# Layer norm of three token blocks taken from the transposed input, and the first raw MLP weights loaded earlier

## The chip, the cores and the metric

The kernel runs on one core of a Trainium2 chip. The metric is device time in microseconds (us) of one execution; lower is better. Before the change three runs took 2244.16 to 2245.52 us, median 2245.15 us.

## The reference, cut to what matters

```python
x = A_x                                        # [2048, 576], fp32
g = sigmoid((x * gate_w).sum(-1))
q, k, v = split(x @ wqkv)                      # 32 heads of 18
a = softmax(q @ k.T * 18 ** -0.5) @ v @ wo
y = (x - mean(x)) / sqrt(var(x) + 1e-5)        # per token
b = gelu(y @ w1 + b1) @ w2 + b2                # 576 -> 4608 -> 576
out = g * a + (1 - g) * b
```

The change is about `y`, the normed input of the MLP, and about the first pieces of `w1` and `w2`.

## The kernel before, in words

Products keep fp32 accuracy by cutting each operand into a rounded high part and a rest (`hh`, `hl`; `big` holds both) and adding three matmuls of the parts.

The program has a first stage of some 215 us, a long loop, and a tail. **The first stage** goes over four blocks of 512 tokens (`tb` 0 to 3; here block 0 to block 3). Each block is a list of 17 groups, g0 to g16 (L872): nine `qk_group`s (L807, 14 matmuls of 128x512 each) and eight `v_group`s (L827, 14 matmuls of 128x288). A group fills one PSUM bank of the pool `ps_a`, which has four. ScalarE copies the bank to the high part, VectorE subtracts it to get the rest (L821, L822), and SyncE stores both.

Between groups, tables of numbers put the other work of the stage:

- `x_chunk` (L747): four transposes on TensorE (`transposed`, L739, one [128 x 128] tile for each 128 tokens), then ScalarE and VectorE make the parts of the transposed input of the *next* block. Five chunks, after g2 to g6.
- `norm` (L776): stages 0 and 1 make mean and variance on VectorE (L784, L785), and stage 1 the reciprocal of the deviation, with one square root on ScalarE (L790 to L797). Stages 2 and 3 sum x times the gate's weights (L802), and normalize the token rows in place (L804). In block 0 they stand after g5 to g8, in blocks 1 and 2 after g2 to g5, in block 3 after g0 to g3.
- `y_chunk` (L762): four more transposes of the normalized rows, then the parts of `y` (L766, L767), stored to `y_scr`. Five chunks, after g12 to g16 in block 0, g8 to g12 in blocks 1 and 2, g5 to g9 in block 3.
- In block 0 alone, the cutting of `wqkv` into parts (L736, L737), by VectorE or GpSimd.
- From block 1 on, the first score rounds of the attention (`next_round`, L223 and L225: a pair of rounds is four matmuls and four row maxima on VectorE), after the odd groups of block 2, for instance.

Each engine works through its instructions in the order in which the code issues them. So a transpose placed after a group runs on TensorE behind that group and ahead of the next one, and when its input isn't there yet, the next group waits with it.

**The raw MLP weights** are loaded by `load_w1` and `load_w2` into one input tile (L346 to L348). The first loads stand at the first `next` of the MLP's generator, after g2 of block 3. ScalarE and GpSimd cut them into parts (`split`, L376; L381 and L385) from g9 of block 3 on.

**The tail** multiplies the attention's output by `wo` in four blocks (L1123). Between its evictions (L1127), `PLAN` (L49) places the steps that scale the next block's output by its denominators: `normed` (L1032), with L1040 on VectorE as its first step.

Of the kernel before, what the change touches and what calls it, by code (L numbers as in the profile page):

```python
# [8 lines left out]
F32 = mybir.dt.float32  # L9
# [40 lines left out]
        [(0,), (1,), (2,), (3,), (4,), (5,), (6,), ()]]  # L50
# [7 lines left out]
N_AT = 5  # L58
W_AT = {0: 1, 1: 2, 2: 3, 4: 4, 6: 5, 7: 6}
# [6 lines left out]
def gated_mix_kernel(ctx: ExitStack, tc: tile.TileContext, x, wqkv, wo, w1, b1, w2, b2, gate_w, out):  # L66
# [17 lines left out]
    b_scr = dram.tile([S, D], F32, name="b_scr")  # L84

# [38 lines left out]
    def x_tile():  # L124
        return xp.tile([P, 4 * 640], F32, name="x")
# [206 lines left out]
    def mlp():  # L332
# [13 lines left out]
        raws = x_tile()  # L346
        R1 = raws[:, :9 * P].rearrange("p (c n) -> p c n", c=9)
        R2 = [raws[:, 9 * P + k * D:9 * P + (k + 1) * D] for k in range(2)]  # L348
# [3 lines left out]
        def load_w1(q):  # L352

            if (1, q) in LOADED or q >= NQ0:
                return
            LOADED[1, q] = slot[0] + LAND
            fc = chunk(q)[2]
            for h in range(2):
                src = w1[:, (fc + h) * P:(fc + h + 1) * P]
                nc.sync.dma_start(R1[64 * h:64 * h + 64], src.rearrange("(c p) n -> p c n", p=64))  # L360

        def load_w2(c):
            if (2, c) in LOADED or c >= NFC:
                return
            LOADED[2, c] = slot[0] + LAND
            nc.sync.dma_start(R2[c % 2], w2[c * P:(c + 1) * P, :])

# [37 lines left out]
        def prep(upto):  # L405

            while asked[0] <= min(upto, npair - 1):
                q = asked[0]
                asked[0] += 1
                shape = [P, 2, 9, P]  # L410
                if q >= NQ0:
                    reload(W1, q, wp1, shape, w1_scr[q % NQ0])
                    continue
                split(W1, q, wp1, shape, (1, q), R1, w1_scr[q], lambda q: load_w1(q + 1))

        def prep_w2(i):
            for m in range(G // 2):
                q = i * (G // 2) + m
                for j in range(2):
# [4 lines left out]
                    split(W2, (q, j), wp2, [P, 2, D], (2, c), R2[c % 2], w2_scr[c],  # L424
# [186 lines left out]
        load_w1(0)  # L611
        for c in range(2):
            load_w2(c)
# [79 lines left out]
    with ExitStack() as a:  # L693
# [10 lines left out]
        glog = wpool.tile([P, NT], F32, name="glog")  # L704

# [41 lines left out]
        def x_chunk(tb, c):  # L747
# [4 lines left out]
            ps = transposed(tb, c)  # L752
            if c < 4:
                nc.scalar.activation(big[:, c, :], ps, AF.Copy)
                nc.vector.tensor_tensor(big[:, 4 + c, :], ps, big[:, c, :].bitcast(F32), op=ALU.subtract)
            else:
# [3 lines left out]
                nc.vector.tensor_tensor(big[64:128, 8, :], ps[64:128], tmp[64:128, :].bitcast(F32), op=ALU.subtract)  # L760

        def y_chunk(tb, c):  # L762
# [5 lines left out]
            for s_, e in enumerate((eh, el)):  # L768
                if c < 4:
                    nc.sync.dma_start(y_scr[tb, s_, 2 * c:2 * c + 2].rearrange("c p n -> (c p) n"), e.bitcast(F32))  # L770
                else:
                    nc.sync.dma_start(y_scr[tb, s_, 8], e[0:64].bitcast(F32))
# [3 lines left out]
        def norm(tb, stage):  # L776
# [21 lines left out]
            if stage >= 2:  # L798
                junk = pp.tile([P, 2, 2, TB], F32, name="p").rearrange("p a b c -> p (a b c)")
                for t in (2 * stage - 4, 2 * stage - 3):  # L800
# [3 lines left out]
                    nc.vector.tensor_scalar(xv[:, t, :], xv[:, t, :], stats[:, tt, 0:1], rstds[tb][:, t:t + 1],  # L804
                                            op0=ALU.subtract, op1=ALU.mult)
# [56 lines left out]
        for i in range(2):  # L862
            for j in range(2):
                nc.gpsimd.memset(KA[i][64 * j + 32:64 * j + 64, :].bitcast(F32), 1.0)
        for c in range(5):
# [5 lines left out]
        for tb in range(NB):  # L871
            work = [(qk_group, (tb, mt)) for mt in (range(9) if tb < 2 else (4, 0, 1, 2, 3, 5, 6, 7, 8))] + [(v_group, (tb, t, n)) for t in range(4) for n in range(2)]  # L872
            for g, (fn, args) in enumerate(work):
# [12 lines left out]
                ng = g - (N_AT, 2, 2, 0)[tb]  # L886
                if 0 <= ng < 4:
                    norm(tb, ng)
                if tb + 1 < NB and 2 <= g < 7:
                    x_chunk(tb + 1, g - 2)  # L890
                yg = g - (12, 8, 8, 5)[tb]
                if 0 <= yg < 5:
                    y_chunk(tb, yg)
                if g == (16 if tb == 0 else 13) and tb + 2 < NB:
                    load_x(tb + 2)
# [342 lines left out]
```

## Time and profile before

| what | value |
|---|---|
| median of three runs | 2245.15 us |
| the profiled execution: its own time | 2244.72 us |
| its span, first to last instruction | 2242.9 us |
| TensorE matmul busy | 2220.6 us, 99% of the span |
| VectorE busy | 1648.7 us, 74% |
| ScalarE busy | 1425.8 us, 64% |
| GpSimd busy | 964.2 us, 43% |
| mean granted TensorE clock | 0.999 |

How to read the rows: PE is TensorE's matmuls, DVE is VectorE, ACT ScalarE, POOL GpSimd, SP SyncE. A row of a timeline has start and duration in us, the engine, the line, the operation, output and input, and in brackets how long the engine stood idle before it and what ended that. A row of the table of stretches has the stretch, its length, the busy time of each engine with the number of instructions, the granted clock (1.00 is full), the share of the DMA engines and GB/s. A row of the table of groups ends with the busy time in us and the mean ns of one.

### The profile page before, as it was taken

To read this page: it belongs to the slowest core of one execution; us is meant where nothing else is said; L and a number is where in the kernel's file an instruction comes from. 1 tells how busy PE (TensorE), PEld (TensorE's weight loads), DVE (VectorE), ACT (ScalarE), POOL (GpSimd) and SP (SyncE) were. 2 spreads that over 40 slices of the span, in tenths; PEclk is the share of its full clock that TensorE was granted. 3 is DMA by queue.
4 is the path that set the end of the run, shared out by engine and by line. 5 is a ranking of instruction groups with operands and counts; after the bars stand their busy time and mean duration, and the time that the engine had idled before them with its cause. 6 is when DMAs were issued, how large, how long until landed. Compare 5 with 4: busy or idle time off the path is not lost.

```text
span 2242.9 us, 51659 instructions
## 1 busy us (share of the span) xinstructions
PE 2220.6 (99%) x20585; PEld 1588.3 (71%) x20585; DVE 1648.7 (74%) x2892; ACT 1425.8 (64%) x2650; POOL 964.2 (43%) x970
## 2 busy tenths in 40 slices
PE   9999999999999999999999999999999999999998
PEld 7887667767666776676676766776766767776768
DVE  5677677777778777777777777777776777777734
ACT  4223677777776666666666666666666666666671
POOL 3001766666665444444444444444444444444700
PEclk9999999999999999999999999999999999999999
DMA  7757654445454624333354424232464334242264
GB/s 249 254 171 239 215 176 128 151 158 174 139 194 146 192 77 145 119 123 105 113 169 145 137 80 135 99 123 99 126 170 144 107 115 124 95 143 99 84 212 167
DMA packets 163624, 327.65 MB, mean 146 GB/s; under 512 B 56742, under 2 KB 83978, under 8 KB 152654
## 3 DMA queue, kind: packets, MB, share of 16 engines
q1 hardware_dynamic: 161286, 320.61, 44.1%
q8 instruction: 162, 2.65, 0.5%
q10 hardware_dynamic: 1968, 3.70, 0.4%
q14 instruction: 80, 0.66, 0.1%
q0 software_dynamic: 128, 0.03, 0.0%
HBM read 231.90 MB, written 96.16 MB: 146 GB/s over the span
## 4 chain that ended last, share of the span: by engine, by line
PE 92%; DVE 2%; DMA 2%; POOL 1%; ACT 1%; SPq 0%; issue 0%; ACTq 0%; DVEq 0%; POOLq 0%
PE ps L281 20%; PE ps L473 20%; PE ps L561 19%; PE ps L263 13%; PE ps L223 11%; PE ps L815 4%; PE ps L836 2%; PE ps L1123 2%; DVE m L225 1%; DMA x<-ot_scr 1%; PE ps L742 1%; DMA low<-ot_scr 0%; POOL zz L176 0%; ACT zz L526 0%; PE ps L818 0%
## 5 line engine op out<-in xcount | busy, mean ns | idle before, releaser
L225 DVE TENSOR_REDUCE m<-ps 128x1 f32<-128x512 f32 x2048 | 1312.3, 685 | 412.0 <-PE ps L223 387.9
L266 ACT ACTIVATE p<-ps 128x512 f32<-128x512 f32 x1368 | 741.2, 596 | 380.2 <-PE ps L263 376.3
L473 PE MATMUL ps<-big,w 64*128 64x512 f32 x3708 | 570.0, 393 | 1.8 <-ACT v L845 1.0
L176 POOL TENSOR_SCALAR zz<-zz 128x512 f32<-128x512 f32 x288 | 178.4, 620 | 752.4 <-ACT zz L526 730.3
L561 PE MATMUL ps<-w,hh 64*128 64x288 f32 x4352 | 485.7, 294 | 4.3 <-DVE x L578 2.4
L266 ACT ACTIVATE ring<-ps 128x512 f32<-128x512 f32 x680 | 369.1, 596 | 190.0 <-PE ps L263 188.4
L263 PE MATMUL ps<-qa,ka 56*128 56x512 f32 x2048 | 461.0, 422 | 2.9 <-ACT p L266 2.4
L561 PEld LDWEIGHTS ps<-w,hh 64*128 64x128 f32 x4352 | 425.6, 186 | 32.6 <-DVE x L578 4.9
L223 PE MATMUL ps<-ka,qa 54*128 54x512 f32 x2048 | 434.8, 398 | 0.7
L473 PEld LDWEIGHTS ps<-big,w 64*128 64x128 f32 x3708 | 370.9, 187 | 66.7 <-ACT v L845 1.3
L176 POOL TENSOR_TENSOR zz<-zz,z 128x512 f32<-128x512 f32 x288 | 371.8, 1291 | 24.0
L263 PEld LDWEIGHTS ps<-qa,ka 56*128 56x128 f32 x2048 | 214.4, 184 | 220.7 <-DVE m L225 180.6
L561 PE MATMUL ps<-w,hl 64*128 64x288 f32 x2176 | 349.2, 292 | 0.8 <-POOL hl L176 0.8
L281 PE MATMUL ps<-p,vt 128*32 128x512 f32 x2560 | 322.8, 598 | 0.0
L223 PEld LDWEIGHTS ps<-ka,qa 54*128 54x128 f32 x2048 | 219.1, 184 | 24.4 <-DVE m L225 3.8
L561 PEld LDWEIGHTS ps<-w,hl 64*128 64x128 f32 x2176 | 232.5, 185 | 1.2 <-POOL hl L176 1.1
L176 POOL TENSOR_TENSOR w<-x,w 128x576 fp32r<-128x576 f32 (+1 forms) x54 | 98.7, 1843 | 294.2 <-ACT w L381 275.0
L176 POOL TENSOR_TENSOR hl<-zz,hh 128x512 fp32r<-128x512 f32 x136 | 176.6, 1299 | 11.4
L281 PE MATMUL ps<-ring,vt 128*32 128x512 f32 x1280 | 168.5, 598 | 0.0
L281 PEld LDWEIGHTS ps<-p,vt 128*32 128x32 f32 x2560 | 67.0, 109 | 142.6 <-issue 136.4
L578 DVE SCALAR_TENSOR_TENSOR x<-ps,x 128x288 f32<-128x288 f32 x256 | 104.1, 448 | 9.6 <-PE ps L561 9.6
L815 PE MATMUL ps<-big,wqk 128*128 128x512 f32 x432 | 109.2, 401 | 0.4 <-DVE wqk L737 0.4
(114 smaller groups left out, 1468.3 us busy)
## 6 DMA issues: line engine op xcount, KB each, us to landing
w<-w_scr SPq DMA_DIRECT2D x54, 1152.0 KB
w<-w_scr SPq DMA_DIRECT2D x108, 576.0 KB
x<-in_B_w_dram SPq DMA_DIRECT2D x72, 288.0 KB
w_scr<-w SPq DMA_DIRECT2D x18, 1152.0 KB
w_scr<-w SPq DMA_DIRECT2D x36, 576.0 KB
qa<-qk_scr SPq DMA_DIRECT2D x192, 72.0 KB
ka<-qk_scr SPq DMA_DIRECT2D x84, 144.0 KB
qk_scr<-hh SPq DMA_DIRECT2D x36, 256.0 KB
```

What stands on the lines that cost most here:

```text
L176: fn(*args, **kw)
L223: nc.tensor.matmul(ps, qa[r0:r0 + 54, t * P:(t + 1) * P], ka[r0:r0 + 54, kb * TB:(kb + 1) * TB], start=True, stop=True)
L225: nc.vector.tensor_reduce(M4[u][:, h, t, kb:kb + 1], ps, axis=AX.X, op=ALU.max)
L263: nc.tensor.matmul(ps[h], ka[r0:r0 + 56, kc * P:(kc + 1) * P], qa[r0:r0 + 56, qb * TB:(qb + 1) * TB], start=True, stop=True)
L266: nc.scalar.activation(RING[n % 3][:, qb, h], ps[h], AF.Exp, scale=SCALE)
L281: nc.tensor.matmul(OB[u][r:r + 32, :], v[:, k, 19 * h:19 * h + 32], RING[c % 3][:, qb, h, :], start=(k == 0), stop=(k == NT - 1))
L473: nc.tensor.matmul(ps[h], wt[w_][r, c, :], y[r, c, :], start=(k == 0), stop=(k == 26))
L561: mm = nc.tensor.matmul(ps[nn][:, :ND], h_[r, tok], w_[p_][r, cs[nn]], start=(k == 0), stop=(k == 6 * G - 1))
L578: nc.vector.scalar_tensor_tensor(dst, ps[nn][:, :ND], 0.5, b2b[:, cs[nn]] if g == 0 else dst, op0=ALU.mult, op1=ALU.add)
L815: nc.tensor.matmul(ps, w_[:, c, ms], big[:, s_, :], start=(k == 0), stop=False)
L836: nc.tensor.matmul(ps[:, :ND], big[:, s_, tok], w_[:, c, cs], start=(k == 0), stop=False)
L1123: nc.tensor.matmul(ps[:, :ND], OT[b][2][:, s_, tok], w_part(w_, c)[:, cs], start=(k == 0), stop=(k == 13))
```

## The change

Block 0 keeps its way, but its five `y_chunk`s move from g12..g16 to g8..g12. For blocks 1 to 3 (one block ahead, that is in the groups of blocks 0 to 2):

- The normalization in place and the five second transposes go. Instead `x_chunk` takes the transposed tile in PSUM, subtracts a row of means on VectorE (line 773 of the changed kernel), and multiplies by a row of reciprocal deviations on GpSimd. Two or three groups later `y_parts` makes the parts, on ScalarE and GpSimd, and they are stored one group after that.
- The rows come from `stat_rows`: two small VectorE copies into `stp`, one TensorE transpose of `stp`, a ScalarE copy and a store to DRAM. `load_wide` then loads the rows back, spread over all partitions, into `QA[2]`, which isn't used yet.
- Statistics stand after g3 and g4 of block 0, and after g0 and g1 of blocks 1 and 2. `stat_rows` stands after g5 of block 0 and g2 of blocks 1 and 2. The `x_chunk`s stand after g12..g16 of block 0, and g5..g9 of blocks 1 and 2. Block 3 has none of this any more.
- The input of block 2 is loaded after g13 instead of g16 of block 0, that of block 3 after g0 instead of g13 of block 1.

The raw MLP weights get two input tiles, and the first four pieces of `w2` and two of `w1` are loaded after g11 of block 2. In the tail, the steps for the last block stand two evictions later.

```diff
 PLAN = [...
-        [(0,), (1,), (2,), (3,), (4,), (5,), (6,), ()]]
+        [(), (), (0,), (1,), (2,), (3,), (4,), (5, 6)]]
...
+BLOCK = [dict(stats=3, rows=5, wide=7, gate=9, x=12, lag=3, load=13),
+         dict(stats=0, rows=2, wide=3, gate=3, x=5, lag=2, load=0),
+         dict(stats=0, rows=2, wide=3, gate=3, x=5, lag=2)]
...
-        raws = x_tile()
+        for raws in (x_tile(), x_tile()):
...
-        load_w1(0)
-        for c in range(2):
-            load_w2(c)
+        for q in range(2):
+            load_w1(q)
+            for c in range(2 * q, 2 * q + 2):
+                load_w2(c)
+        yield 1
...
             ps = transposed(tb, c)
+            if tb > 0:
+                if c == 0:
+                    yT[tb] = pp.tile([P, 2, 2, TB], F32, name="p").rearrange("p a b c -> p (a b) c")
+                y = yT[tb][:, c % 4, :]
+                nc.vector.tensor_tensor(y, ps, wide[:, 0, :], op=ALU.subtract)
...
+            if tb > 0:
+                nc.gpsimd.tensor_tensor(y, y, wide[:, 1, :], op=ALU.mult)
...
+        def y_parts(tb, c):
+            y = yT[tb][:, c % 4, :]
+            eh = hp.tile([P, TB], F32R, name="hh")
+            el = hp.tile([P, TB], F32R, name="hl")
+            nc.scalar.activation(eh, y, AF.Copy)
+            nc.gpsimd.tensor_tensor(el, y, eh.bitcast(F32), op=ALU.subtract)
+            after(1, lambda: y_store(tb, c, eh, el))
...
+        def stat_rows(tb):
+
+            nc.vector.tensor_copy(stp[:, 0:4], stats[:, 4 * tb:4 * tb + 4, 0])
+            nc.vector.tensor_copy(stp[:, 4:8], rstds[tb])
+            ps = psum(ps_a)
+            nc.tensor.transpose(ps[:, :P], stp, ident)
+            nc.scalar.activation(strow, ps[:8, :P], AF.Copy)
+            nc.sync.dma_start(st_scr[tb], strow)
+
+        def load_wide(tb):
+            rows = bcast_rows(st_scr[tb], 8 * P)
+            nc.sync.dma_start(wide, rows.rearrange("p (a n) -> p a n", a=2))
...
-                    nc.vector.tensor_scalar(xv[:, t, :], xv[:, t, :], stats[:, tt, 0:1], rstds[tb][:, t:t + 1],
-                                            op0=ALU.subtract, op1=ALU.mult)
+                    if tb == 0:
+                        nc.vector.tensor_scalar(xv[:, t, :], xv[:, t, :], stats[:, tt, 0:1], rstds[tb][:, t:t + 1],
+                                                op0=ALU.subtract, op1=ALU.mult)
...
+                if tb == 0:
+                    if 0 <= g - N_AT < 4:
+                        norm(0, g - N_AT)
+                    if 0 <= g - 8 < 5:
+                        y_chunk(0, g - 8)
...
+                    if g in (at["stats"], at["stats"] + 1):
+                        norm(tb + 1, g - at["stats"])
+                    if g == at["rows"]:
+                        stat_rows(tb + 1)
```

How the instructions stand now. Names are as in the code, except that buffer numbers follow some of them (`wqk_125` is a part of the qk weights, `wv_127` of the v weights). The line numbers of the first list of each pair are those of the kernel before, of the second those of the changed one. First TensorE in block 0, from the end of g5 into g6; before, with a chunk of block 1's input between them:

```order
L815 MATMUL ps<-big,wqk_125 128x512
L817 MATMUL ps<-big,wqk_124 128x512
L818 MATMUL ps<-big,wqk_125 128x512
L742 MATMUL ps<-ident,x 128x128 x4
L815 MATMUL ps<-big,wqk_124 128x512 x2
```

And now:

```order
L879 MATMUL ps<-big,wqk_126 128x512
L881 MATMUL ps<-big,wqk_125 128x512
L882 MATMUL ps<-big,wqk_126 128x512
L829 MATMUL ps<-ident,stp 128x128
L879 MATMUL ps<-big,wqk_125 128x512 x2
```

The transposes of an input tile, loaded long before, have left, and the transpose of `stp` (L829) stands in their place. VectorE at the same place, from the eviction of g5 on; before, with the first half of block 0's statistics behind it, then the rest part of the input chunk:

```order
L822 TENSOR_TENSOR hl<-ps,hh 128x512
L784 BN_STATS st_377<-x 128x6 x2
L785 BN_AGGR stats<-st_377 128x2
L784 BN_STATS st_381<-x 128x6 x2
L785 BN_AGGR stats<-st_381 128x2
L755 TENSOR_TENSOR big<-ps,big 128x512
L822 TENSOR_TENSOR hl<-ps,hh 128x512
```

And now:

```order
L886 TENSOR_TENSOR hl<-ps,hh 128x512
L847 BN_STATS st_385<-x 128x6 x2
L848 BN_AGGR stats<-st_385 128x2
L847 BN_STATS st_389<-x 128x6 x2
L848 BN_AGGR stats<-st_389 128x2
L826 COPY stp<-stats 128x4
L827 COPY stp<-rstd 128x4
L886 TENSOR_TENSOR hl<-ps,hh 128x512
```

The copies into `stp` (L826, L827) stand behind the eviction of g5 and behind that first half of block 0's own statistics. Last, TensorE from the end of g8 on; before, the v groups g9 and g10 follow at once:

```order
L815 MATMUL ps<-big,wqk_125 128x512
L817 MATMUL ps<-big,wqk_124 128x512
L818 MATMUL ps<-big,wqk_125 128x512
L836 MATMUL ps<-wv_126,big 128x288
L836 MATMUL ps<-wv_127,big 128x288
```

And now:

```order
L881 MATMUL ps<-big,wqk_125 128x512
L882 MATMUL ps<-big,wqk_126 128x512
L758 MATMUL ps<-ident,x 128x128 x4
L900 MATMUL ps<-wv_127,big 128x288
L900 MATMUL ps<-wv_128,big 128x288
```

The first four transposes of block 0's normalized rows (L758) moved from behind g12 to behind g8, whose issue also carries the last stage of `norm` on VectorE.

More of the change, by code (lines that the diff above doesn't have):

```diff
@@ L767, in y_chunk, with after, next_turn @@
             nc.vector.tensor_tensor(el, ps, eh.bitcast(F32), op=ALU.subtract)
[L768 to L772, printed above, removed]
+            y_store(tb, c, eh, el)
+        turn = [0]
+        queued = []
+        def after(n, fn):
+            queued.append((turn[0] + n, fn))
+        def next_turn():
+            turn[0] += 1
+            due = [f for t, f in queued if t <= turn[0]]
+            queued[:] = [(t, f) for t, f in queued if t > turn[0]]
+            for f in due:
+                f()
+        def stat_rows(tb):
[8 more added lines that the diff above has]
+            nc.sync.dma_start(wide, rows.rearrange("p (a n) -> p a n", a=2))
         rstds = {}
```

54 lines of the change are left out of this document (38 added, 16 removed).

## The prediction

> **What bounds the kernel now.** I read the page's busy times first, then the stretches, to see where TensorE has idle time at all. The first four stretches are blocks 0 to 3 of the first stage, the fifth is the start of the loop, the last is the tail.
>
> ```profile
> 9.10:58.84 49.74, 49.38 (x280) 42.62 (x279) 29.73 (x58) 22.55 (x38) 10.92 (x5) 1.00 0.80 257
> 58.84:110.80 51.96, 51.96 (x296) 43.86 (x295) 33.24 (x70) 13.74 (x30) 0.00 (x0) 1.00 0.74 250
> 110.80:167.50 56.70, 56.49 (x313) 45.54 (x312) 42.87 (x86) 14.41 (x30) 0.00 (x0) 1.00 0.51 174
> 167.50:221.00 53.50, 53.50 (x296) 43.16 (x294) 41.46 (x89) 19.87 (x33) 5.68 (x4) 1.00 0.75 238
> 221.00:345.00 124.00, 118.63 (x1091) 80.12 (x1092) 86.53 (x146) 86.76 (x159) 82.39 (x73) 1.00 0.57 183
> 2130.00:2242.90 112.90, 105.29 (x839) 82.60 (x835) 45.98 (x84) 51.47 (x99) 3.36 (x4) 0.98 0.56 191
> ```
>
> TensorE (the first busy time) fills the four blocks to within 0.4 us each. So a matmul or transpose removed there is time gained in full, and a TensorE wait added there is time lost in full. Idle time is left only at the loop's start (5.4 us) and in the tail (7.6 us).
>
> Next, the timeline of TensorE in block 1, with ScalarE's and VectorE's rows for the group that ends at 65.46:
>
> ```profile
> 62.20 2.96 PE L815 MATMUL ps<-big,wqk 128*128 128x512 f32 x12
> 65.46 2.96 PE L815 MATMUL ps<-big,wqk 128*128 128x512 f32 x12
> 68.73 0.60 PE L742 MATMUL ps<-ident,x 128*128 128x128 f32 x4
> 69.08 3.05 PE L815 MATMUL ps<-big,wqk 128*128 128x512 f32 x12
> 72.79 3.04 PE L815 MATMUL ps<-big,wqk 128*128 128x512 f32 x12
> 65.66 0.60 ACT L821 ACTIVATE hh<-ps 128x512 fp32r<-128x512 f32 x1 [2.67 <-PE ps L818]
> 66.29 0.69 DVE L822 TENSOR_TENSOR hl<-ps,hh 128x512 fp32r<-128x512 f32 x1 [2.58 <-ACT hh L821]
> ```
>
> A qk group takes 3.27 us (65.46 to 68.73), and one with a chunk's four transposes 3.71 (69.08 to 72.79): a chunk costs 0.44. VectorE starts a group's eviction 0.83 us after TensorE has gone on (66.29 against 65.46).
>
> **The change part by part.**
>
> *Transposes.* Fifteen chunks go: 15 x 0.44 = 6.6 us. Three transposes of `stp` come, a quarter of a chunk each: 0.3. Net -6.3 us.
>
> *The transposes of `stp`.* Each stands on TensorE between two groups, and needs two VectorE copies that stand behind the eviction of the group just finished. So the next group, queued behind the transpose, can't start before that eviction. Before the change TensorE had no such wait. How long it is depends on what else VectorE has to do. These rows have the durations, from blocks 0 and 2:
>
> ```profile
> 114.24 2.96 PE L815 MATMUL ps<-big,wqk 128*128 128x512 f32 x12
> 118.26 3.06 PE L815 MATMUL ps<-big,wqk 128*128 128x512 f32 x12
> 123.06 0.81 DVE L784 BATCH_NORM_STATS2 st<-x 128x6 f32<-128x288 f32 x2
> 124.96 0.64 DVE L755 TENSOR_TENSOR big<-ps,big 128x512 fp32r<-128x512 f32 x1
> 126.76 0.81 DVE L784 BATCH_NORM_STATS2 st<-x 128x6 f32<-128x288 f32 x2
> 130.13 0.66 DVE L755 TENSOR_TENSOR big<-ps,big 128x512 fp32r<-128x512 f32 x1
> 130.71 2.48 DVE L225 TENSOR_REDUCE m<-ps 128x1 f32<-128x512 f32 x4
> 133.09 0.68 DVE L822 TENSOR_TENSOR hl<-ps,hh 128x512 fp32r<-128x512 f32 x1
> 133.69 0.75 DVE L802 SCALAR_TENSOR_TENSOR p<-x,gwb 128x576 f32<-128x576 f32 x1
> L790 DVE TENSOR_SCALAR var<-stats 128x4 f32<-128x4 f32 x4 | 0.7, 170 | 0.1
> 16.59 2.96 PE L815 MATMUL ps<-big,wqk 128*128 128x512 f32 x12
> 26.34 0.87 ACT L736 ACTIVATE wqk<-p 128x800 fp32r<-128x800 f32 x1 [1.49 <-DMA p<-in_A_wqkv_dram]
> 39.40 1.40 ACT L736 ACTIVATE wv<-p 128x1440 fp32r<-128x1440 f32 x1
> 40.83 1.66 DVE L737 TENSOR_TENSOR wv<-p,wv 128x1440 fp32r<-128x1440 f32 x1 [0.55 <-ACT wv L736]
> 43.13 0.75 DVE L802 SCALAR_TENSOR_TENSOR p<-x,gwb 128x576 f32<-128x576 f32 x1
> 45.78 0.69 DVE L822 TENSOR_TENSOR hl<-ps,hh 128x512 fp32r<-128x512 f32 x1
> ```
>
> From start to start: the first half of the statistics 1.90 us (123.06 to 124.96), the second half with the square root 3.37 (126.76 to 130.13), four row maxima 2.38 (130.71 to 133.09), an eviction 0.60 (133.09 to 133.69), half of block 0's normalization 2.65 (43.13 to 45.78). A pair of rounds adds 0.75 to TensorE's group (114.24 to 118.26 is 4.02). The two copies aren't in the trace. The nearest row, 128x4 elements in 170 ns, gives 0.4 us for both with their spacing, my value. The bounds are 0.34 (no spacing) and 1.2 (two evictions), which moves the three waits together by -0.2 to +2.4.
>
> Block 0: g2 starts at 16.59, so g5 ends at 16.59 + 4 x 3.27 = 29.7. VectorE: g3's eviction is done at 23.1 + 1.4 = 24.6, block 1's first half of statistics at 26.5. ScalarE is held until 27.2 by a weight copy that waits for its DMA (26.34), so g4's eviction ends at 28.4, the second half at 31.75, g5's eviction at 32.4, block 0's first half (issued between them) at 34.3, the copies at 34.7. TensorE waits from 29.7 to 34.7: **5.0 us**.
>
> Block 1: counted from its start, g1's eviction ends at 6.6 + 1.4 = 8.0, the second half of the statistics at 11.4, g2's eviction at 12.0, the copies at 12.4. TensorE has finished g2 at 9.85: **2.6 us**.
>
> Block 2: the same to 11.4, then four row maxima to 13.75, eviction and copies to 14.8. TensorE has finished g2 at 9.85 + 0.8: **4.1 us**.
>
> *The `y_chunk`s of block 0.* They start behind g8, whose issue also carries the last half of the normalization, so their third and fourth transpose, and g9 behind them, wait for it. g6 starts at 34.85, g8 ends at 44.65. VectorE: g6's eviction to 39.5, the second half to 42.9. The last cut of weights comes behind it, as its ScalarE copy (1.40) stands behind the square root: copy to 43.1, VectorE's 1.66 to 44.8. Then g7's eviction to 45.4, 2.65 to 48.05, g8's eviction to 48.65, 2.65 to 51.3. TensorE waits from 44.65 to 51.35: **6.7 us**. Before, the chunks stood four groups later, and TensorE came there as the rows were ready.
>
> The four waits have a floor where VectorE has no arrears: the eviction (1.4) and what is issued ahead of the copies or the transposes, which is 3.75, 1.9, 1.9 and 4.1, together 11.65 us. My sum is 18.4 us; I take it, as every arrear in it follows from rows.
>
> *The clock.* Two rows before show what a wait of TensorE can bring, the first at 2141, the second at 2214 us:
>
> ```profile
> 2141.13 0.89 PE L561 MATMUL ps<-w,hh 64*128 64x288 f32 x4 [1.45 <-DVE x L578]
> 2214.77 1.60 PE L1123 MATMUL ps<-big 128*128 128x288 f32 x10 [2.06 <-DVE res L1127]
> 2140.00:2145.00 5.00, 3.87 (x33) 3.69 (x35) 4.98 (x10) 2.52 (x5) 0.76 (x1) 0.75 0.16 37
> 2145.00:2150.00 5.00, 5.00 (x55) 3.36 (x53) 3.85 (x7) 5.00 (x11) 1.12 (x1) 0.91 0.57 179
> 2215.00:2220.00 5.00, 5.00 (x39) 5.00 (x39) 4.87 (x10) 2.31 (x5) 0.00 (x0) 1.00 0.80 256
> ```
>
> After a wait of 1.45 us the granted clock was 0.75 and 0.91 over ten microseconds: 5 x 0.25 + 5 x 0.09 = 1.7 us lost. After one of 2.06 us it stayed at 1.00. I count 1.7 us for each of the two longest waits, +3.4; between 0 and 4 x 1.7 = 6.8 is possible. The Trainium skill's "TensorE: Matmul & The Clock Gate" (section "What's actually happening") has the clock halved after an idle window of about 3.4 us, and back after as much busy time. By that rule three of my waits would pay, +5.1 in place of +3.4 and 2258.6 us in the sum below; the trace, with its drop after 1.45 us, doesn't keep to the threshold.
>
> *VectorE, ScalarE, GpSimd.* VectorE's subtraction of the mean replaces the one in `y_chunk`, and the normalization in place goes, in three blocks. GpSimd gets two operations of 512 elements a chunk. It has no work at all in blocks 1 and 2 (0.00 busy), so these are hidden; they cost something only if more than the 3.7 us of a group. The broadcast rows have over three groups (10 us) from `stat_rows` to their first use in blocks 1 and 2, and more in block 0: nothing on the path.
>
> *Raw weights.* At the end of the stage ScalarE waits for raw weights, and TensorE for ScalarE:
>
> ```profile
> 220.01 0.69 ACT L381 ACTIVATE w<-x 128x576 fp32r<-128x576 f32 x1 [4.76 <-DMA x<-in_B_w_dram]
> 222.49 0.97 PE L473 MATMUL ps<-big,w 64*128 64x512 f32 x6 [0.99 <-ACT v L845]
> 224.59 0.49 PE L263 MATMUL ps<-qa,ka 56*128 56x512 f32 x1 [0.68 <-ACT p L266]
> ```
>
> Loaded a block sooner, the weights are there: -0.99 - 0.68 = -1.65 us. At least 0 (what is late next is the v store ahead of L845), at most the 5.4 us of idle time in that stretch.
>
> *The tail.* TensorE's 2.06 us at 2214.77 come from this VectorE wait, in front of an eviction:
>
> ```profile
> 2208.49 0.37 PE L1123 MATMUL ps<-big 128*128 128x288 f32 x1 [0.41 <-DVE big L1052]
> 2213.60 0.69 DVE L1040 TENSOR_TENSOR x<-x,den 128x512 f32<-128x512 f32 x1 [4.04 <-DMA x<-ot_scr]
> ```
>
> Two evictions later the load has landed. What is late next is the last part of that block, which the same table costs 0.41 us at 2208.49 already: -2.06 + 0.41 = -1.65.
>
> **Sum:** -6.3 + 18.4 + 3.4 - 1.65 - 1.65 = +12.2 us on the profiled 2244.72, which is 0.4 under the median: 2257.
>
> **The rivals.** I call no change what lies within 0.2% (4.5 us), about what a measurement here can tell.
>
> *VectorE keeps up* (not slower). If VectorE stands idle when each eviction comes, the four waits are at their floor and none is long enough to cost clock: -6.3 + 11.65 - 3.3 = +2.05, or 2247. For it: VectorE is busy only 30 of 50 us in block 0. Against: in block 0 its work comes in one lump behind weights that land at 26.34, and 5.3 us of statistics are moved into that lump, for 5 x 0.6 of chunks that leave it. It decides where the four waits together fall under 14.1 us (9.6 + 4.5). For faster they would have to fall under 5.1, which the order doesn't allow; only the loop's idle 5.4 us, gone whole, with the floor and no clock loss, gets to -1.7, and a clock drop in the tail that doesn't recur (1.45 + 1.7) to -4.9. Chances: no change 0.13, faster 0.05.
>
> *Rows or buffers late* (slower still). `load_wide` stands on SyncE behind stores that wait for GpSimd. If its rows land three microseconds after TensorE's need in blocks 1 and 2, VectorE stops in front of the evictions, and TensorE after four banks: up to +6, 2263. Against: the 10 us of slack. 0.10.
>
> *The raw weights change nothing*, the conversions being paced by the loop's own slots: 2258.6. 0.12.
>
> **How the numbers follow.** The forecast, 2257, has 0.60; with its clock term at 0 it is 2253.6, at 6.8 2260.4. The range goes from the floor, 2247, to late rows with some more clock loss, 2264. Slower by over 0.2%: 0.60 + 0.10 + 0.12 = 0.82.
>
> **What would show it.** In the changed kernel's profile: a wait of TensorE before each of the three transposes of `stp` (5.0, 2.6, 4.1 us, released by VectorE's copy), one before block 0's first normalized transposes (6.7, released by the normalization); block 0 some 12 us longer, block 3 two shorter; granted clock under 1 behind the long waits; no wait at L845 or at L1127. Waits under 2 us each, or a first stage that ends earlier than at 221 us, would make the forecast wrong.

## The result, and the profile after

The changed kernel takes **2263.82 us** (median of six runs, 2263.04 to 2265.41); the kernel before took 2244.89 us beside it. The ratio is 1.0085, with a 95% interval of 1.0072 to 1.0098: slower by 19 us, where 12 were forecast (2257.0, range 2247 to 2264). The profiled execution took 2265.41 us, with a span of 2263.6 against 2242.9.

First the stretches of the changed kernel: blocks 0 to 3, the loop's start and the tail. The columns are those of the same table above; the first busy time is TensorE's, and the granted clock stands before the last two columns.

```profile
9.50:73.91 64.41, 54.19 (x280) 46.06 (x279) 39.55 (x89) 24.04 (x40) 15.80 (x10) 0.92 0.75 239
73.91:129.92 56.01, 52.83 (x279) 43.25 (x277) 33.34 (x70) 16.33 (x35) 20.38 (x17) 0.97 0.75 248
129.92:191.14 61.22, 57.16 (x294) 45.23 (x293) 40.86 (x84) 13.30 (x28) 12.74 (x10) 0.94 0.51 161
191.14:247.69 56.55, 52.97 (x274) 41.66 (x272) 29.90 (x52) 20.83 (x33) 10.87 (x6) 0.97 0.66 203
247.69:371.00 123.31, 119.51 (x1109) 82.22 (x1110) 88.44 (x151) 86.17 (x157) 78.64 (x70) 1.00 0.56 177
2150.00:2263.60 113.60, 108.90 (x895) 84.84 (x887) 47.81 (x90) 54.08 (x104) 7.08 (x9) 1.00 0.56 191
```

All the loss is in the first stage, which ended at 220.99 us and now ends at 247.69: +26.7. Loop and tail give 6.0 of it back (26.7 - 20.7). Every block has idle time of TensorE now (10.2, 3.2, 4.1 and 3.6 us), and a clock under 1. Block 0 is 14.7 us longer than before, where some 12 were forecast, and block 3 is 3.1 longer, where it was to be two shorter.

The waits of TensorE in that stage, with the sum, the count and the longest:

```profile
PE ps L829 <- DVE stp L827: 11.0, 3, 4.1
PE ps L758 <- DVE x L868: 5.7, 4, 2.3
PE ps L879 <- ACT v L909: 3.6, 1, 3.6
PE ps L484 <- DVE vt L911: 1.2, 1, 1.2
```

The first two were forecast: the transposes of `stp` (L829) and block 0's normalized transposes (L758). The third, in block 3, was not. The timeline of TensorE shows the five places, and what the next group took:

```profile
34.57 0.48 PE L829 MATMUL ps<-ident,stp 128*128 128x128 f32 x1 [4.09 <-DVE stp L827]
34.70 4.27 PE L879 MATMUL ps<-big,wqk 128*128 128x512 f32 x12
39.27 2.96 PE L879 MATMUL ps<-big,wqk 128*128 128x512 f32 x12
...
52.73 0.48 PE L758 MATMUL ps<-ident,x 128*128 128x128 f32 x1 [0.85 <-DVE x L868]
52.86 3.23 PE L900 MATMUL ps<-wv,big 128*128 128x288 f32 x12
...
87.28 0.30 PE L829 MATMUL ps<-ident,stp 128*128 128x128 f32 x1 [3.06 <-DVE stp L827]
87.33 4.41 PE L879 MATMUL ps<-big,wqk 128*128 128x512 f32 x12
...
144.58 0.45 PE L829 MATMUL ps<-ident,stp 128*128 128x128 f32 x1 [3.85 <-DVE stp L827]
144.68 5.47 PE L879 MATMUL ps<-big,wqk 128*128 128x512 f32 x12
...
201.40 4.53 PE L879 MATMUL ps<-big,wqk 128*128 128x512 f32 x12 [3.58 <-ACT v L909]
```

Twelve matmuls take 2.96 us at full clock (39.27). Behind the waits they take 4.27, 4.41, 5.47 and 4.53, and the smaller ones of a v group 3.23 in place of 1.85. With the rows that follow each, the waits cost 1.3, 2.35, 1.6, 2.5 and 1.6 us of slow clock: 9.4 in all.

The wait at 201.40 begins on SyncE. Its queue in the changed kernel, at the end of block 2 and the start of block 3:

```profile
183.96 2.04 SPq L371 DMA_DIRECT2D x<-in_B_w_dram  x2
...
189.61 1.99 SPq L377 DMA_DIRECT2D x<-in_B_w_dram  x2
191.72 0.36 SPq L914 DMA_DIRECT2D v_scr<-vt  x1
...
195.86 5.86 SPq L914 DMA_DIRECT2D v_scr<-vt  x2
```

The eight raw loads, now behind g11 of block 2, take SyncE's time from 183.96 to 191.6, ahead of the stores of `v` of block 2's last groups. ScalarE then has no free buffer for the next one:

```profile
200.85 0.42 ACT L907 ACTIVATE vt<-ps 128x288 f32<-128x288 f32 x1 [16.23 <-DMA v_scr<-vt]
```

It waits 16.23 us for a store to finish, and TensorE, out of banks, 3.58 us for it.

In the tail the 2.06 us before L1127 are gone and a wait of 0.42 us stands in their place, as forecast; also the wait of 1.45 us at 2141, with its slow clock, is gone, which was not.

### The profile page after: what moved, and what is told of

It reads as the page before. It is cut to its first block, busy times and chain, and to the rows that moved or that the text cites. A ratio compares the mean times of both kernels' runs of the same rounds, so it can differ in the third digit from the quotient of the medians.

```text
span 2263.6 us, 51585 instructions
## 1 busy us (share of the span) xinstructions
PE 2224.4 (98%) x20528; PEld 1585.9 (70%) x20528; DVE 1646.2 (73%) x2886; ACT 1428.2 (63%) x2653; POOL 1002.5 (44%) x1001
## 4 chain that ended last, share of the span: by engine, by line
PE 87%; DVE 2%; ACT 1%; DMA 1%; issue 1%; POOL 1%; SPq 0%; ACTq 0%; POOLq 0%
PE ps L285 20%; PE ps L572 19%; PE ps L484 19%; PE ps L267 13%; PE ps L227 10%; PE ps L1202 3%; PE ps L879 2%; DVE m L229 1%; PE ps L900 1%; DMA x<-in_B_w_dram 1%; ACT zz L537 0%; DMA v_scr<-vt 0%; POOL w L180 0%; SPq L371 0%; ACT p L270 0%
## 5 line engine op out<-in xcount | busy, mean ns | idle before, releaser
L227 PE MATMUL ps<-ka,qa 54*128 54x512 f32 x2048 | 434.2, 398 | 0.8
L227 PEld LDWEIGHTS ps<-ka,qa 54*128 54x128 f32 x2048 | 218.5, 185 | 25.9 <-DVE m L229 5.5
L879 PE MATMUL ps<-big,wqk 128*128 128x512 f32 x432 | 115.7, 418 | 4.1 <-ACT v L909 3.6
```

The lines of the kernel that those rows point to most:

```text
L227: nc.tensor.matmul(ps, qa[r0:r0 + 54, t * P:(t + 1) * P], ka[r0:r0 + 54, kb * TB:(kb + 1) * TB], start=True, stop=True)
L879: nc.tensor.matmul(ps, w_[:, c, ms], big[:, s_, :], start=(k == 0), stop=False)
```

## The experiments

Twelve kernels ran. None leaves work out; one adds some. The kernel before took 2244.71 to 2245.23 us (medians) beside them.

### Raw weights at their old place

```diff
-                if tb == 2 and g == 11:
-                    next(stream[0])
...
                     if g == 2:
                         load_q(1)
                         next(stream[0])
+                        next(stream[0])
```

> The changed kernel with the raw MLP weights loaded at the old place (after g2 of block 3). Theory A, each TensorE wait of the first stage costs its length and a stretch of slow clock: the 3.6 us wait of block 3 and its 1.6 us of clock go, ScalarE's wait for a v store falls from 16 us to under 3, and at most 1.7 us come back at the loop's start, so 2259 to 2260 us. Rival B, the early loads help more than they hurt: 2264 to 2267 us, with ScalarE's wait for raw weights back at 4 us or more and TensorE's wait at the loop's start over 1.5 us.

Measured: 2260.24 us (2257.89 to 2261.54), ratio 1.0068 (1.0053 to 1.0083). Block 3, in the table of stretches:

```profile
191.35:242.60 51.25, 51.25 (x275) 40.63 (x273) 29.92 (x52) 19.57 (x31) 10.85 (x6) 1.00 0.74 218
```

It takes 51.25 us, 2.2 below before (53.50), near the two that the forecast gave it, without idle time and at full clock: the wait of block 3 is the raw loads' doing. Of the 5.1 us that the stage gains, 3.6 reach the end in the medians; the profiled run shows a clock of 0.67 at the loop's start, which takes some 1.7. It stands behind waits of 1.15 and 0.6 us; the same waits in the changed kernel cost no clock.

### The transposes of the rows two groups later

```diff
-            ps = psum(ps_a)
-            nc.tensor.transpose(ps[:, :P], stp, ident)
+            def turned():
+                ps = psum(ps_a)
+                nc.tensor.transpose(ps[:, :P], stp, ident)
...
+            after(2, turned)
```

`load_wide` and, in blocks 1 and 2, the `x_chunk`s stand two groups later with it, and the raw loads behind g12 instead of g11.

> The changed kernel with the transpose of stp two groups behind its copies, and load_wide and the chunks two groups later to match. Theory A: the three waits (4.4, 3.3, 4.1 us) and their clock (1.3, 1.6, 2.5 us) go, 17 us in all, so 2246 to 2249 us; the wait for block 0's normalized rows stays at 6 us or more. Rival C, VectorE's arrears are the bound and the wait only moves on to the next PSUM bank or the next transpose: less than 6 us gained, 2258 us or more.

Measured: 2248.57 us (2247.49 to 2250.61), ratio 1.0015 (1.0006 to 1.0025), 15.3 below the changed kernel. The two edits share this: of the 16.1 us by which the first stage is shorter, 4.6 are in block 3, where the raw loads were the trouble, and 11.5 in blocks 0 to 2, less than the 17 expected. The waits of TensorE in the first stage:

```profile
PE ps L758 <- DVE x L871: 7.0, 4, 3.7
PE ps L227 <- DVE m L229: 1.5, 2, 0.9
```

No wait at a transpose of `stp` is left: the copies needed time, not TensorE's next slot. The wait for block 0's normalized rows stayed, as expected, and is longer than before (7.0 us against 5.7). Raw loads only one group later no longer stop the `v` stores either. But a small new wait appears in block 1, at a pair of score rounds (L227), as `x_chunk`s now stand in the short v groups:

```profile
113.44 2.28 PE L227 MATMUL ps<-ka,qa 54*128 54x512 f32 x4 [0.56 <-DVE m L229]
115.65 2.39 PE L903 MATMUL ps<-wv,big 128*128 128x288 f32 x12
118.31 2.58 PE L903 MATMUL ps<-wv,big 128*128 128x288 f32 x12
```

The four matmuls of the rounds take 2.28 us in place of 0.73, and the clock falls behind them (2.39 and 2.58 in place of 1.85).

### Block 0's normalized transposes later, and all three together

```diff
-BLOCK = [dict(stats=3, rows=5, wide=7, gate=9, x=12, lag=3, load=13),
-         dict(stats=0, rows=2, wide=3, gate=3, x=5, lag=2, load=0),
+BLOCK = [dict(stats=3, rows=5, wide=7, gate=9, x=12, lag=3, load=16),
+         dict(stats=2, rows=4, wide=5, gate=5, x=7, lag=2, load=0),
...
-                    if 0 <= g - 8 < 5:
-                        y_chunk(0, g - 8)
+                    if 0 <= g - 12 < 5:
+                        y_chunk(0, g - 12)
```

> The changed kernel with block 0's normalized chunks behind g12 to g16 as before, and block 1's steps two groups later to match. Theory A: the wait for the normalized rows (6.6 us) and its clock (2.3 us) go, 2254 to 2256 us. Rival C, VectorE's work of block 0 is the bound wherever the chunks stand: the wait stays over 4 us or turns up at the input chunks, 2259 us or more.

Measured: 2262.41 us (2261.81 to 2264.33). That is rival C's figure, but not by its signs: the wait at block 0's chunks is gone and block 1 begins 5.4 us sooner, and still the time hardly moves. The stretches of blocks 0 and 1:

```profile
9.50:68.52 59.02, 52.57 (x280) 44.24 (x280) 38.94 (x89) 23.51 (x40) 17.28 (x12) 0.97 0.73 236
68.52:127.75 59.23, 54.94 (x275) 45.03 (x276) 33.07 (x70) 16.57 (x36) 18.93 (x15) 0.94 0.80 260
```

Block 1 takes 59.23 us in place of 56.01. Block 2's input is loaded later there, so block 1's steps had to move by two groups, into the v groups. A pair of score rounds there takes 2.29 us in place of 0.73, and the granted clock is 0.66 from 120 to 125 us, behind it.

All three edits in one kernel (block 1's rows loaded behind g7, its chunks behind g9 to g13):

> The three edits together: raw weights at the old place, stp's transpose two groups behind its copies, block 0's chunks behind g12. Theory A: the five waits of the first stage and all of its slow clock go, some 31 us, with up to 1.7 us back at the loop's start: 2233 to 2236 us, that is faster than the kernel before by the 6.3 us of transposes and what the tail and the loop gained. Rival C: 2245 us or more, the first stage no shorter than before the change.

Measured: 2250.78 us (2249.54 to 2255.66), far above theory A; the figure is rival C's, and so is the first stage, which is no shorter than before the change. TensorE's longest waits are 3.4 and 3.3 us in blocks 1 and 0, and block 1 takes 61.5 us. What stops block 1 is the rows of block 2, which come late. SyncE's, VectorE's and TensorE's rows there:

```profile
98.45 0.29 SPq L833 DMA_DIRECT2D st_scr<-strow  x1
...
101.41 0.32 SPq L838 DMA_DIRECT2D qa<-st_scr  x1
...
105.88 0.69 DVE L773 TENSOR_TENSOR p<-ps,qa 128x512 f32<-128x512 f32 x1 [7.05 <-DMA qa<-st_scr]
...
108.07 1.09 PE L758 MATMUL ps<-ident,x 128*128 128x128 f32 x4 [3.36 <-DVE big L776]
```

ScalarE had copied the rows at 91.35 us, but SyncE issued their store only at 98.45, behind twelve loads into `qa` and `ka`, and the load at 101.41. VectorE stands idle for 7.05 us until the rows land, and TensorE for 3.36 us behind it; the granted clock is 0.69 and 0.63 over the ten microseconds from 105 us. This is the prediction's rival of late rows, in a kernel where the edits made them later. In block 0 VectorE's first use of the rows, at 53.19 us, has no wait ahead of it. The gains of the two edits so far do not add up.

### The order of two reads of one bank

ScalarE's table of waits had a line that no part of the prediction holds: its copy of the transposed bank (L775) waits for VectorE's subtraction (L773), which reads the same bank. VectorE's rows in the changed kernel:

```profile
65.82 0.68 DVE L773 TENSOR_TENSOR p<-ps,qa 128x512 f32<-128x512 f32 x1
67.17 0.69 DVE L776 TENSOR_TENSOR big<-ps,big 128x512 fp32r<-128x512 f32 x1 [0.67 <-ACT big L775]
67.78 0.68 DVE L773 TENSOR_TENSOR p<-ps,qa 128x512 f32<-128x512 f32 x1
```

VectorE stands idle for 0.67 us in each chunk, while ScalarE copies; and when VectorE is in arrears, ScalarE's copy is in arrears with it. The experiment, on the kernel with the rows apart, issues the copy first:

```diff
             ps = transposed(tb, c)
-                nc.vector.tensor_tensor(y, ps, wide[:, 0, :], op=ALU.subtract)
...
+                nc.vector.tensor_tensor(y, ps, wide[:, 0, :], op=ALU.subtract)
                 nc.gpsimd.tensor_tensor(y, y, wide[:, 1, :], op=ALU.mult)
```

> The kernel with the rows apart (2248.6), but VectorE's subtraction of the mean stands behind ScalarE's copy and VectorE's rest instead of ahead of them. Theory A (two engines' reads of one PSUM tile are done one after the other in the order of issue): ScalarE's waits for VectorE at the copy (10 of them, 18.2 us) go, and so does VectorE's 0.67 us of idle time before most rests; TensorE hardly waits there, so the time stays within 2 us, 2246.5 to 2248.6. Rival B (ScalarE is late for other reasons): the waits stay and so does the time. Rival C: the subtraction now keeps GpSimd and the bank longer, TensorE waits, 2250 or more.

Measured: 2244.15 us (2243.07 to 2245.52), ratio 0.9996 (0.9987 to 1.0006), 4.4 below the kernel with the rows apart: more than theory A gave it. ScalarE's 18.2 us of waits for VectorE are gone. The stretches of blocks 0 to 3:

```profile
9.50:70.08 60.58, 53.19 (x281) 45.39 (x280) 40.45 (x88) 23.58 (x41) 15.51 (x10) 0.92 0.76 245
70.08:120.87 50.79, 50.69 (x278) 42.32 (x277) 33.73 (x71) 16.12 (x36) 20.71 (x17) 1.00 0.84 283
120.87:175.00 54.13, 54.03 (x293) 43.20 (x292) 40.68 (x84) 15.51 (x32) 12.63 (x10) 1.00 0.55 177
175.00:227.00 52.00, 51.23 (x272) 40.49 (x271) 29.43 (x51) 18.53 (x30) 10.85 (x6) 1.00 0.73 224
```

Blocks 1 to 3 take 156.9 us against 162.2 before the change. The 6.3 us of transposes that the prediction counted come out at 5.2, once next to nothing waits. The wait for VectorE at the rounds of block 1 is gone. Block 0 keeps its 61 us.

### Three waits put into the kernel before

```diff
+HOLD = {(1, 0): 0, (2, 0): 2, (3, 0): 6}
...
+        def hold(n):
+            for _ in range(n):
+                nc.vector.tensor_copy(spin, spin)
+            nc.vector.tensor_copy(spin[:, :P], spin[:, :P])
+            ps = psum(ps_a)
+            nc.tensor.transpose(ps[:, :P], spin[:, :P], ident)
...
+                if (tb, g) in HOLD:
+                    hold(HOLD[tb, g])
```

> The kernel before with three waits put in, nothing else: after the first group of blocks 1, 2 and 3 VectorE copies a small tile, with 0, 2 and 6 further copies ahead, and TensorE transposes it. By the eviction (1.4 us) and copies of 0.2 to 0.5 us each, TensorE waits about 1.6, 2.3 and 3.7 us, 7.6 in all, and the transposes take 0.3. Theory A (every wait over 1.4 us costs some 1.7 us of slow clock, as after the wait at 2141): 7.9 + 5.1 over 2244.9, 2258. Theory B (only waits over about 3.4 us cost clock): 7.9 + 1.7, 2254.5, with the granted clock at 1.00 behind the first two. Theory C (no clock lost, what TensorE did ahead of the wait decides): 2253.

Measured: 2254.03 us (2253.41 to 2257.07). The waits were 1.64, 2.43 and 4.00 us, 8.1 in all. The stretches behind each, and then the group behind the third:

```profile
65.00:70.00 5.00, 5.00 (x23) 4.00 (x23) 0.69 (x1) 0.60 (x1) 0.00 (x0) 1.00 0.85 279
120.00:125.00 5.00, 5.00 (x24) 3.55 (x23) 1.93 (x4) 0.60 (x1) 0.00 (x0) 1.00 0.23 80
180.00:185.00 5.00, 5.00 (x13) 3.98 (x13) 1.43 (x5) 0.00 (x0) 0.00 (x0) 0.50 0.00 0
185.00:190.00 5.00, 5.00 (x21) 3.98 (x21) 2.92 (x10) 1.11 (x3) 0.00 (x0) 0.93 0.35 117
```

```profile
179.87 5.46 PE L825 MATMUL ps<-big,wqk 128*128 128x512 f32 x12
```

Only the third cost clock: 5 x 0.5 + 5 x 0.07 = 2.85 us. That is theory B. The sum would be 8.1 + 0.3 + 2.85 = 11.2 where 9.2 were measured; the wait of 1.45 us at 2141, which in this kernel is 0.8 us, with the clock at 1.00 behind it (0.65 + 1.7 less), makes up for the difference.

### The tail's table alone

```diff
 PLAN = [...
-        [(0,), (1,), (2,), (3,), (4,), (5,), (6,), ()]]
+        [(), (), (0,), (1,), (2,), (3,), (4,), (5, 6)]]
```

> The kernel before, with only the table of the tail changed (the steps for the last block two evictions later). Theory A, as predicted: the wait of 2.06 us at L1127 goes and 0.41 us comes in its place, 2243.2 us, and the slow clock at 2141 us stays, since nothing there is touched. Rival B: the wait only moves to the next eviction, no change, 2244.9. Rival C: the wait of 1.45 us at 2141 and its slow clock belong to the tail's table too and go with it, 1.65 + 1.45 + 1.7 less, 2240.1.

Measured: 2241.06 us (2239.95 to 2244.79, 11 runs), ratio 0.9985 (0.9976 to 0.9994): 3.8 us less, between A and C. In its trace the wait at L1127 is replaced by two of 0.4 us, and the wait at 2141 by one of 0.6 with the clock at 1.00. That this wait is also shorter, and without slow clock, with the three waits put in, where the table is the old one, speaks against the table as its cause; it is a wait that comes and goes with the kernel's timing. The granted clock of the single executions says the same. At equal mean clock the new table saves 2.0 us (at 1.000), 1.65 (0.999) and 2.2 (0.998), near theory A's 1.65; the rest of the 3.8 is that six of its 11 executions ran at 1.000, and only five of 27 of the kernel before. The profiled run is the longest of the 11: it has a wait of 1.9 us at the loop's start and this behind it:

```profile
226.00:231.00 5.00, 5.00 (x26) 3.82 (x26) 1.57 (x3) 2.09 (x5) 2.13 (x1) 0.50 0.96 303
```

### The new way for two blocks only

Blocks 0 and 1 are made as before (block 1's normalization and its chunks two groups sooner), blocks 2 and 3 by the new way with the rows apart; first with VectorE's subtraction ahead of the copy, then behind it.

```diff
-BLOCK = [dict(stats=3, rows=5, wide=7, gate=9, x=12, lag=3, load=13),
-         dict(stats=0, rows=2, wide=3, gate=3, x=5, lag=2, load=0),
-         dict(stats=0, rows=2, wide=3, gate=3, x=5, lag=2)]
+BLOCK = [dict(),
+         dict(stats=4, rows=5, wide=9, gate=12, x=12, lag=2),
+         dict(stats=0, rows=2, wide=5, gate=3, x=7, lag=2)]
...
-            if tb > 0:
+            if tb > 1:
```

> Blocks 2 and 3 get their normed input by the new way, blocks 0 and 1 by the old one; the transpose of the rows stands two groups behind its copies, and the raw weights load after g12. Theory A (the added waits come from block 0, where VectorE has no room left): block 0 takes 49.7 us as before, block 1 about 52 and some small waits, blocks 2 and 3 what they took with the rows apart (55.9 and 52.0), the first stage ends about 2 us sooner than before, and with the 5.9 us that loop and tail give back the time is 2237 (2234 to 2240), faster than the kernel before. Rival B (VectorE is short of room in whichever block makes two blocks' statistics, now block 1 with 16 us of them in its first six groups): TensorE waits 3 us or more in block 1, with slow clock behind, 2242 to 2248.

Measured: 2245.59 us (2244.48 to 2248.36), ratio 1.0007 (0.9998 to 1.0015), rival B's figure. Block 0 took the expected 49.5 us, but TensorE waited 2.1 us at the first group of block 2, with a clock of 0.66 behind it; rival B had put 3 us or more in block 1.

> The new way for blocks 2 and 3 only, now with ScalarE's copy of the transposed bank issued first. Theory A (block 1's waits came from ScalarE and VectorE taking turns on that bank): block 0 takes 49.5 us as with the new way for two blocks, block 1 52.1 as before the change, blocks 2 and 3 54.1 and 52.0 as with the copy first, so the stage ends at 217.2, 3.8 before the kernel before; with 3.4 from the tail's table 2237.7 (2235 to 2240), faster than both kernels. Rival B (VectorE has too much to do in block 1): a wait of 2 us or more and slow clock in block 1 as without the copy first, 2242 or more.

Measured: **2236.61 us** (2235.78 to 2238.22), ratio 0.9964 (0.9951 to 0.9976): faster than both kernels. Its blocks 0 to 3:

```profile
9.50:58.99 49.49, 49.31 (x280) 42.74 (x278) 29.45 (x58) 22.31 (x37) 10.74 (x6) 1.00 0.79 255
58.99:112.15 53.16, 52.95 (x299) 44.48 (x297) 41.68 (x98) 14.34 (x32) 5.25 (x4) 1.00 0.79 262
112.15:167.08 54.93, 54.37 (x295) 43.21 (x293) 44.02 (x89) 17.64 (x37) 20.36 (x17) 1.00 0.63 212
167.08:219.16 52.08, 51.74 (x275) 40.82 (x273) 29.91 (x52) 19.06 (x31) 10.85 (x6) 1.00 0.74 227
```

No wait over 0.5 us, no slow clock. VectorE has the same work in block 1 as in the kernel with the subtraction ahead (41.68 us against 41.24), so block 1's waits there came from the order of the two reads, not from too much work.

### Block 0's transposes later, with the copy first

Both have the rows apart and the copy first. The one has block 0's chunks behind g11 to g15, block 2's input loaded after g16 and block 1's steps one group later; the other the chunks behind g10 to g14 and the load after g14.

```diff
-                    if 0 <= g - 8 < 5:
-                        y_chunk(0, g - 8)
+                    if 0 <= g - 11 < 5:
+                        y_chunk(0, g - 11)
```

> The kernel with the rows apart and the copy first (2244.2), block 0's y chunks behind g11 to g15 instead of g8 to g12, block 2's input loaded at g16, block 1's steps one group later. Theory A (block 0's wait for the normalization is all that is left there): 7.0 us of waits and 4.3 us of slow clock go; the rows land at about 53 us by the other runs, 4 us after VectorE can first use them, of which TensorE sees 2 to 4: 2235 to 2237. Rival B (with the late rows and the later steps the arrears move into block 1, as without the copy first): 2241 or more, with waits of VectorE for the rows over 5 us and of TensorE at the end of block 0 or in block 1.

Measured: 2241.17 us (2240.77 to 2242.79), ratio 0.9985 (0.9976 to 0.9994). Theory A's figure is missed by 4 us. Rival B's figure is met, and its signs nearly: VectorE waits 4.7 us for the rows of block 2, in block 1 at 99.54 us, and TensorE 1.6 us behind it. The 53 us in the expectation were VectorE's first use in the kernel with all three edits, for which it had not waited. Block 1 takes 52.9 us at full clock, where the shifted steps had cost 59 to 61 without the copy first. At block 0's chunks two waits are left, 1.11 and 0.99 us, and the granted clock of block 0 is 1.00.

> The same kernel (rows apart, copy first, 2244.2) with block 0's y chunks behind g10 to g14 and block 2's input loaded after g14, nothing else. Theory A (each group of 128x288 matmuls ahead of the chunks takes 1.87 us from the wait): the wait of 3.7 at the first chunk goes, 3.3 of 7.0 us stay, without a wait of 3 us on end the slow clock goes too: 3.7 + 4.3 less, 2236 (2234 to 2239). Rival B (the rows are late for g12's chunk): VectorE waits for them 2 us or more and TensorE with it, and the clock drops there, 2241 or more.

Measured: 2240.52 us (2239.50 to 2243.50), ratio 0.9981 (0.9972 to 0.9990). The waits came out at 3.4 us, where 3.3 were expected, and VectorE did not wait for the rows, as rival B had it; but the clock fell all the same. TensorE's rows:

```profile
45.21 0.33 PE L758 MATMUL ps<-ident,x 128*128 128x128 f32 x1 [1.00 <-DVE x L871]
47.13 0.48 PE L758 MATMUL ps<-ident,x 128*128 128x128 f32 x1 [1.59 <-DVE x L871]
48.45 0.47 PE L758 MATMUL ps<-ident,x 128*128 128x128 f32 x1 [0.85 <-DVE x L871]
48.58 3.23 PE L903 MATMUL ps<-wv,big 128*128 128x288 f32 x12
...
52.80 2.14 PE L903 MATMUL ps<-wv,big 128*128 128x288 f32 x12
```

Three waits of at most 1.59 us with single transposes between them cost as much clock as one long wait: by the starts of the rows, the v group behind them took 3.51 us where one takes 1.95 at full clock, and with the transposes and the group that follow, 2.2 us are lost. From the first of these transposes to the next group TensorE did nothing else for 4.7 us (43.88 to 48.58); in the kernel before this one, with two waits, it was 2.9 us, and that cost no clock.

### The fastest kernel with the raw weights at their old place

```diff
-                if tb == 2 and g == 12:
-                    next(stream[0])
...
                         next(stream[0])
+                        next(stream[0])
```

> The fastest kernel so far (2236.6), with the raw weights loaded where they were before the change, after g2 of block 3, still into two tiles. Its first stage ends 1.8 us sooner than before the change, the tail's table gave 3.4 to 3.8, and 8.1 were gained: some 2.5 are open. Theory A, as predicted (raw weights sooner take a wait off the loop's start): they are the raw weights', and the time becomes 2238.3 to 2239. Rival B (the loop's start is paced by the last v eviction, whatever the weights do): no change, 2236.6 within 0.7.

Measured: 2236.12 us (2235.33 to 2237.09), ratio 0.9963 (0.9949 to 0.9976): no change, rival B. The loop's start has the same wait of 1.2 us for VectorE's v eviction in both. Of the 2.5 us that were open, none are the earlier place of the loads; whether the second input tile brings them was not tried.

## Why the prediction was right, and where not

Direction and main mechanism were right: the first stage pays with waits of TensorE for what it saves in transposes. The size was 7 us short. That the range held is luck: the result lies 0.2 us inside its top, and the top had been set for late rows, which this kernel doesn't have; the clock and the raw weights brought the time there. By its steps:

- **Transposes, -6.3.** Nearly right. Blocks 1 to 3 take 5.2 us less than before where next to nothing waits (the copy first); in the changed kernel the gain is buried.
- **The transposes of `stp`, 5.0, 2.6 and 4.1 us.** Right. By the starts of the rows they cost 4.4, 3.3 and 4.1: 11.8 against 11.7. That the sum is so near is luck, as the first two are off by 0.6 and 0.7 in opposite ways. Moving TensorE's part two groups away took away all three, as their cause demands.
- **Block 0's normalized transposes, 6.7 us.** Right: 6.6 (from the end of g8 at 45.81 to 52.86, less the 0.44 of the transposes themselves). In block 0 the last normalization began at 52.06 us, forecast for about 51.
- **The clock, +3.4.** This term was mis-sized: it measured +9.4. The step that failed is "I count 1.7 us for each of the two longest waits": all five waits paid, 1.3 to 2.5 us each. The four that were forecast cost 7.8, more than the 6.8 that I had called possible, and the fifth, in block 3, 1.6. I had let one wait of 2.06 us that cost nothing speak for waits of 2.6 to 5 us. In the kernel before with three waits put in, 2.43 us cost nothing and 4.00 us cost 2.85. The Trainium skill's "TensorE: Matmul & The Clock Gate" (section "What's actually happening") has the clock halved after an idle window of about 3.4 us, in windows that run freely. By that rule 1.64, 2.43 and 4.00 us there and 4.09, 3.85 and 3.58 here come out right, and so does a wait of 3.27 us in block 0 of the kernel with all three edits, which cost none; but 3.06 us paid here, and shorter waits in other places did too (1.45 us at 2141 in the kernel before, 1.9 us at the loop's start). The rule's 2258.6 was nearer than my sum, and still short, as it had no fifth wait.
- **Raw weights, -1.65.** Wrong in sign. I wrote "at least 0", and named the v store as what is late next, at the loop's start. In fact the eight loads stand on SyncE ahead of block 2's last v stores, and cost a wait of 3.58 us and 1.6 of clock in block 3. At the loop's start the 0.68 us are gone and the 0.99 became 1.16, for VectorE's v eviction (L911); with the loads at the old place, but still two tiles, it is the same, so the earlier place gained nothing there. At the old place, or one group later, that wait is gone; and in the fastest kernel the place of the loads is worth nothing at all. The step that failed is that I read the gain at the place where the data is used, and didn't walk SyncE's queue at the place where the loads are issued.
- **VectorE, ScalarE, GpSimd, 0.** Incomplete. Their work is hidden, but the order of ScalarE's copy and VectorE's subtraction on one bank is not: 4.4 us between two kernels that differ in it alone.
- **The rows, 0.** Right for this kernel, in which VectorE never waits for them, but with luck in block 1: SyncE issues the load at 95.40 us and VectorE uses the rows at 100.25, 4.85 later. Where the transposes of `stp` stand two groups later, VectorE waited for the rows in block 1 in three kernels (1.1, 7.1 and 4.7 us), and began 4.5 to 5.9 us after the load's issue. I had named SyncE's queue as a rival's cause, but counted the 10 us of slack as if it were free.
- **The tail, -1.65.** Right as read (2.06 against 0.42). The wait at 2141 and its clock, 1.45 + 1.7, went too; I had taken them as fixed, but they are 0 to 0.8 us and no clock in the other kernels' traces.

From the parts: -6.3 + 11.8 + 6.6 + 9.4 + 3.7 (block 3's wait) = 25.2 of the 26.7 us; the rest is in two pairs of score rounds that are stretched by about 1 us each.

## What to carry to other kernels

A transpose or any small TensorE instruction that depends on the group just finished costs the whole eviction and whatever else its producer has queued; put two groups between the producer and it, and check that what hangs on its result still comes in time. When loads are moved earlier, read the issuing queue at the new place, for what stands behind them there, before reading the gain at the place of use. When TensorE must wait, price the slow clock with the wait: here some 1.3 to 2.9 us for most waits of 3 us or more, and for three short ones in a row with nothing but transposes between them.

## What the runs showed of the hardware that was not expected

- **Two readers of one PSUM bank take turns.** ScalarE's copy starts only when VectorE's read of the same bank is over, although neither changes it: 13.7 us of such waits in the changed kernel, 30.2 in the one with all three edits (6.8 of them behind the late rows). The Trainium skill's "PSUM — Partial Sum Buffer" (section "PSUM bank collisions raise a hardware error") says that two engines must not access one bank at the same time, reads included, and that the compiler's scheduler makes them wait for each other; the trace agrees as to the wait (VectorE's read at 65.82 takes 0.68 us, ScalarE's begins at 66.54), and doesn't show what orders it. So the reader on which more depends should be issued first.
- **The clock doesn't go by the length of one wait alone.** Single waits of 1.64 and 2.43 us cost nothing, nor did one of 3.27 us (all three edits, block 0); one of 3.06 us cost 1.6 us of clock, a trio of 1.00, 1.59 and 0.85 cost 2.2 us, and behind a wait of 1.9 us at the loop's start the clock was halved in the longest of 11 runs. What else it depends on is left open.
- **A small row takes long through memory.** In block 1 of the kernel with all three edits, 14.5 us pass from ScalarE's copy (91.35 us) to VectorE's first use (105.88): 7.1 until a busy SyncE queue issues the store, 3.0 to the issue of the load, and 4.5 until VectorE goes on. I had called 10 us slack.
